# FFN tile zero of block 0 in batch columns among the AV groups; q of batches 0 and 1 in single loads, k of batch 1 moved from SP to the software ring; output weights loaded ahead of block 1's q and k

## The chip, the cores and the metric

The kernel runs on one core of one Trainium2 chip. The metric is the device time of an execution in microseconds (us). Each measurement has several executions; medians are quoted. A profiled execution gives a span that is 1.7 to 1.8 us shorter than its device time, and all times "at x us" below are counted from the start of such a span. Instruction counts and clocks come from one profiled execution per kernel.

Engines: PE is TensorE (matrix products), DVE is VectorE, ACT is ScalarE, POOL is GpSimd, SP is SyncE.

## The reference, cut to what matters

The reference is a decayed linear attention over 4 batches, 8 heads, 768 positions of 64 channels, followed by a gated FFN on the 3072 x 512 result:

```python
for b in range(nb):                                   # blocks along the sequence, one after the other
    intra = einsum('bhic,bhjc->bhij', qb, kb) * Dmask       # scores, masked by lam ** (i - j)
    intra = einsum('bhij,bhjd->bhid', intra, vb)            # "AV"
    inter = einsum('bhid,bhde->bhie', qb * lam_pow, kv_state)
    out[:, :, sl] = intra + inter
    kv_state = lam_block * kv_state + einsum('bhsd,bhse->bhde', kb_dec, vb)
# x = out, transposed to (tokens, 512)
gate = sigmoid(x @ w_gate)                            # 512 -> 1536
return (gate * (x @ w_val)) @ w_out                   # 1536 -> 512
```

The kernel works on six blocks of 128 positions, all four batches of a block together. So one block is 512 tokens: its FFN has 12 tiles of gate and value products (`gp`, `vp`: 8 matmuls of 128x512 each tile) and four output products (`po`: 12 matmuls each, one per batch).

## The kernel before

Cuts are marked with `...`. The loads at the start. `load` and `load_gv` are issued by POOL, into one queue whose descriptors POOL writes (the software ring); they cast FP32 to BF16 on the way. `load_hw` is issued by SP without a cast, so DVE casts afterwards.

```python
    load_hw("k", 0, nc.sync)                 # k of block 0, batch 0: FP32 by SP
    load_hw("k", 1, nc.sync)                 # batch 1
    nc.scalar.dma_start(out=lam_bc, ...)
    load(0, "q", 0, 2)                       # q of block 0, batches 0-1: ring
    ...                                      # memsets on DVE; a select for the identity on POOL
    nc.gpsimd.iota(ip1, ...)                 # table work on POOL
    load(0, "k", 2, 4)
    ...                                      # two more iotas, the triangle select
    load(0, "q", 2, 4)
    load(0, "v", 0, 2)
    load(0, "v", 2, 4)
    load_gv(0, 1); load_gv(1, 2); load_gv(2, 4); load_gv(4, 6)   # WG and WV, by tiles of 128 columns
```

The start on the engines: transposes of q and k (`tq`, `tk`), decay of q on DVE (`QS`), copy of k on ACT (`KS`), scores (`sp`), mask product on DVE (`MT`), AV (`op`), copy to the FFN's input (`XT`). `zeros(m)` are m filler matmuls that keep PE busy while it waits.

```python
    for b in range(2, 4):
        piece_s(0, [b]); piece_m(0, b)
    for b in range(2):
        piece_a(0, [b]); piece_x(0, [b], nc.scalar)
    zeros(3)
    piece_a(0, [2]); piece_x(0, [2], nc.scalar)
    zeros(1)
    piece_a(0, [3]); piece_x(0, [3], nc.vector)
    zeros(2)
```

Tile 0 of the FFN then needs all four batches of XT. The later loads, and the order of work for block 0 and block 1 (`trans`: transposes; `att`: AV and XT; `piece_c`: state update products; `kd`: decay of k):

```python
    load_gv(6, 8)
    load(1, "k", 0, 2); load(1, "q", 0, 2)
    load_gv(8, 10)
    load(1, "k", 2, 4); load(1, "q", 2, 4)
    load_gv(10, 12)
    load(1, "v")
    load_wo(0, 6); load_wo(6, 12)
    load(2, "kq")
    ...
    behind[7] = [trans(1, 0)]                # block 1's attention behind FFN tiles 7 to 11 of block 0
    behind[8] = [pair(piece_s, 1, 0), m_(1, 0), m_(1, 1)]
    behind[9] = [trans(1, 1), kd(1, 0)]
    behind[10] = [pair(piece_s, 1, 1), m_(1, 2), m_(1, 3), kd(1, 2), kd(1, 4)]
    behind[11] = [kd(1, 6), att(1), pair(piece_c, 1, 0), pair(piece_c, 1, 1)]
    for ft in range(NFT):
        gv(0, ft, *behind[ft])
    ...                                      # block 1: gv(1, 0..3), then po(0, 0..3), then gv(1, 4..11)
```

PSUM has five buffers for attention (two per batch of scores, one per batch of AV) and three for the FFN.

## Time and profile before

| | before |
|---|---|
| device time, median | 232.91 us (232.73 to 232.94) |
| span of the profiled execution | 231.2 us |
| PE busy | 221.5 us, 96% |
| gate product of tile 0, block 0, starts | 16.52 us |
| gate product of tile 1, block 0, starts | 18.24 us |
| first gate product of block 1 | 44.55 us |
| first output product of block 1 | 79.56 us |

The top of the profile page of the kernel before:

```profile
span 231.2 us, 3734 instructions
PE 221.5 (96%) x1483; PEld 110.6 (48%) x1508; DVE 109.5 (47%) x183; ACT 92.8 (40%) x175; POOL 47.0 (20%) x55
```

PE is nearly always busy. What can be won is in the first 17 us, where PE waits or runs filler, and in single waits later. The timeline of PE in the kernel before, at the last transposes of block 0's inputs and at the first FFN tiles (columns: start, duration, engine, line, operation, out<-in, shapes, count, and in brackets the idle time before it and what ended it):

```profile
10.85 0.62 PE L178 MATMUL tq<-ident,qb 128*128 128x128 bf16 x8 [0.39 <-DMA qb<-in_q_dram]
...
16.52 1.02 PE L273 MATMUL gp<-XT,WG 128*128 128x512 bf16 x4 [0.34 <-DVE XT L246]
17.38 1.03 PE L279 MATMUL vp<-XT,WV 128*128 128x512 bf16 x4
18.24 1.03 PE L273 MATMUL gp<-XT,WG 128*128 128x512 bf16 x4
```

Tile 0 waits for the last XT cast; then a tile takes 1.73 us. The same view where block 1's attention ends:

```profile
39.26 0.62 PE L216 MATMUL sp<-QS,KS 64*128 64x128 bf16 x16
39.81 1.04 PE L273 MATMUL gp<-XT,WG 128*128 128x512 bf16 x4
...
41.55 1.06 PE L230 MATMUL op<-QS,Sb 128*128 128x128 bf16 x16
42.53 1.08 PE L236 MATMUL op<-MT,vb 128*64 128x128 bf16 x32
43.55 1.07 PE L252 MATMUL cp<-vb,kd 128*128 128x128 bf16 x16
44.55 1.02 PE L273 MATMUL gp<-XT,WG 128*128 128x512 bf16 x3
```

Between the last scores (39.26) and AV (41.55) stands FFN tile 11. It gives DVE time for the mask products, so AV, the state products and block 1's first gate product follow without a gap: 3.00 us from 41.55 to 44.55. Duration columns overlap because matmuls are pipelined; read the starts.

The transfers, from the DMA view of the kernel before, 3 to 12 us in 40 slices of 0.225 us (first line: busy share of the 16 DMA engines; second: GB/s written):

```profile
DMA  5999999999999999999999999999999999999999
GB/s 130 213 273 291 288 288 258 203 187 177 170 158 157 158 153 153 146 152 155 160 156 155 158 155 155 151 160 158 158 155 155 158 155 155 158 159 155 156 154 155
```

SP's two loads of k run first. From 5.5 us on the ring alone moves about 155 GB/s (146 to 170).

### The profile page before, as it was taken

The page shows a single profiled execution, that of the slowest core. Times are in us where ns is not written, and L with a number is a line of the kernel's source. Part 1 is how long each engine was busy: PE and PEld are TensorE (multiplying, and loading weights), DVE is VectorE, ACT ScalarE, POOL GpSimd, SP SyncE. Part 2 cuts the span into 40 slices and gives each one's busy share as a digit, 9 for nine tenths or more (in the row PEclk, how much of TensorE's full clock was granted, in tenths as well). Part 3 has the DMA queues.
Part 4 walks back from the last instruction along what each step waited for, and adds up shares of the span by engine and source line. Part 5 has one row for each costly group of instructions (what it writes and reads, how often), then busy time and mean ns, then how long its engine had stood idle before and what let it go on. Part 6 is the DMA issues. An engine that isn't in the chain of part 4 may idle for free.

```text
span 231.2 us, 3734 instructions
## 1 busy us (share of the span) xinstructions
PE 221.5 (96%) x1483; PEld 110.6 (48%) x1508; DVE 109.5 (47%) x183; ACT 92.8 (40%) x175; POOL 47.0 (20%) x55
## 2 busy tenths in 40 slices
PE   6889999999999999999999999999999999999993
PEld 2544555644444644444644544644544554444442
DVE  3963668971068401978300978400778600333300
ACT  5557347532225823347433327442333342433220
POOL 7977672000530080026000030000000000000000
PEclk9999999999999999999999999999999999999999
DMA  7999999999799889969922967012100002100022
GB/s 114 156 176 195 173 173 176 207 168 174 209 166 164 170 94 189 224 129 114 157 53 108 209 43 52 1 45 94 45 0 0 3 35 101 48 0 0 0 91 93
DMA packets 103473, 25.15 MB, mean 109 GB/s; under 512 B 93600, under 2 KB 100512, under 8 KB 103456
## 3 DMA queue, kind: packets, MB, share of 16 engines
q0 software_dynamic: 80992, 13.90, 77.0%
q1 hardware_dynamic: 22320, 11.01, 18.5%
q8 instruction: 12, 0.20, 0.3%
q14 instruction: 5, 0.04, 0.0%
q10 hardware_dynamic: 144, 0.00, 0.0%
HBM read 28.32 MB, written 6.29 MB: 150 GB/s over the span
## 4 chain that ended last, share of the span: by engine, by line
PE 78%; DMA 13%; DVE 3%; POOL 3%; issue 2%; POOLq 0%
PE po L290 27%; PE vp L279 22%; PE gp L273 21%; DMA WV<-in_moe_w_val_dram 10%; DMA vb<-in_v_dram 3%; PE op L236 2%; PE sp L216 2%; DVE Sb L260 2%; PE op L230 2%; PE cp L252 2%; DVE ht L282 1%; POOL qb L78 1%; POOL vb L78 0%; POOL kb L78 0%; POOL WV L85 0%
## 5 line engine op out<-in xcount | busy, mean ns | idle before, releaser
L282 DVE TENSOR_TENSOR ht<-sg,vp 128x512 bf16<-128x512 bf16 x72 | 49.4, 687 | 102.6 <-PE vp L279 101.0
L279 PE MATMUL vp<-XT,WV 128*128 128x512 bf16 x282 | 73.4, 379 | 1.0 <-DMA WV<-in_moe_w_val_dram 0.3
L273 PE MATMUL gp<-XT,WG 128*128 128x512 bf16 x277 | 72.8, 379 | 0.9 <-DVE XT L246 0.3
L276 ACT ACTIVATE sg<-gp 128x512 bf16<-128x512 f32 x72 | 43.0, 597 | 74.1 <-PE gp L273 72.0
L290 PE MATMUL po<-WO,ht 128*128 128x512 bf16 (+1 forms) x294 | 62.7, 370 | 0.4 <-issue 0.2
L279 PEld LDWEIGHTS <-WV 128*128 128x128 bf16 x288 | 28.0, 98 | 34.8 <-DMA WV<-in_moe_w_val_dram 0.9
L290 PEld LDWEIGHTS <-ht 128*128 128x128 bf16 x300 | 29.0, 98 | 32.5
L273 PEld LDWEIGHTS <-WG 128*128 128x128 bf16 x288 | 26.8, 98 | 31.4 <-issue 1.8
L295 ACT COPY ob<-po 128x512 f32<-128x512 f32 (+1 forms) x24 | 13.9, 578 | 45.7 <-PE po L290 45.7
L224 DVE TENSOR_TENSOR MT<-sp,mask 128x512 bf16<-128x512 f32 x48 | 30.4, 682 | 0.6 <-PE sp L216 0.5
L98 ACT ACTIVATE kd<-kb,kds 128x256 bf16<-128x256 bf16 x40 | 17.8, 497 | 0.0
L260 DVE SCALAR_TENSOR_TENSOR Sb<-Sb,dec,cp 64x256 bf16<-64x256 bf16 x32 | 15.3, 478 | 0.8
L361 POOL COPY gates<-kt 128x1 bf16<-128x1 bf16 x4 | 0.8, 188 | 69.9 <-DMA kt<-kb 69.9
L246 ACT CAST XT<-op 128x512 bf16<-128x512 f32 x21 | 11.0, 596 | 7.1 <-PE op L236 7.0
L78 POOL DMA_DIRECT2D qb<-in_q_dram x8 | 11.5, 1441 | 3.5 <-issue 1.6
L78 POOL DMA_DIRECT2D vb<-in_v_dram x7 | 10.7, 1533 | 2.6 <-issue 1.4
L78 POOL DMA_DIRECT2D kb<-in_k_dram x7 | 10.2, 1459 | 1.5 <-DMA WV<-in_moe_w_val_dram 0.7
L304 PE MATMUL zps<-Sb 128*128 128x512 bf16 x22 | 7.8, 482 | 2.1 <-DVE Sb L123 2.1
L236 PE MATMUL op<-MT,vb 128*64 128x128 bf16 x192 | 7.1, 221 | 0.4 <-DVE MT L224 0.4
L236 PEld LDWEIGHTS <-vb 128*64 128x64 bf16 x192 | 5.7, 109 | 1.6 <-DMA vb<-in_v_dram 0.4
L252 PEld LDWEIGHTS <-kd 128*128 128x128 bf16 x80 | 5.1, 98 | 2.0
L252 PE MATMUL cp<-vb,kd 128*128 128x128 bf16 x80 | 5.9, 219 | 0.1
(42 smaller groups left out, 77.3 us busy)
## 6 DMA issues: line engine op xcount, KB each, us to landing
out_dram<-ob SPq DMA_DIRECT2D x23, 256.0 KB, 2.0
vb<-in_v_dram POOLq DMA_DIRECT2D x5, 512.0 KB, 7.9
kb<-in_k_dram POOLq DMA_DIRECT2D x4, 512.0 KB, 10.6
qb<-in_q_dram POOLq DMA_DIRECT2D x4, 512.0 KB, 12.7
WO<-in_moe_w_out_dram POOLq DMA_DIRECT2D x2, 768.0 KB, 16.7
WG<-in_moe_w_gate_dram POOLq DMA_DIRECT2D x5, 256.0 KB, 9.6
WV<-in_moe_w_val_dram POOLq DMA_DIRECT2D x5, 256.0 KB, 10.2
qb<-in_q_dram POOLq DMA_DIRECT2D x4, 256.0 KB, 8.4
```

What stands on the lines that cost most here:

```text
L78: nc.gpsimd.dma_start(out=T_[c, n][:, b0:b1], in_=src[b0:b1, :, sl, :].rearrange("b h s d -> s (b h) d"))
L98: nc.scalar.mul(KD[n][:, :, h, :], T_["k", n][:, :, h, :], kds[:, h:h + 1])
L224: nc.vector.tensor_tensor(out=MT[n, b][:, u], in0=SP[n, b][u], in1=mask[:, u], op=ALU.mult)
L236: nc.tensor.matmul(OP[n, b][us, hp, :], lhsT=T_["v", n][:, b, 2 * hp + u, :], rhs=MT[n, b][:, u, hp, :], start=(n == 0 and hp == 0), stop= ...
L252: nc.tensor.matmul(cp[:, b, :], lhsT=KD[n][:, b, 2 * hp:2 * hp + 2, :], rhs=T_["v", n][:, b, 2 * hp:2 * hp + 2, :], start=(b == 0), stop=( ...
L260: nc.vector.scalar_tensor_tensor(out=Sb[us, :, hp, us], in0=Sb[us, :, hp, us], scalar=dec[us, hp:hp + 1], in1=cp[us, :, us], op0=ALU.mult, ...
L273: nc.tensor.matmul(gp, lhsT=WG[:, mt, fs], rhs=x[:, mt, :], start=(mt == 0), stop=(mt == NMT - 1))
L276: nc.scalar.activation(sg, gp, AF.Sigmoid)
L279: nc.tensor.matmul(vp, lhsT=WV[:, mt, fs], rhs=x[:, mt, :], start=(mt == 0), stop=(mt == NMT - 1))
L282: nc.vector.tensor_mul(HT[n, ft], sg, vp)
L290: nc.tensor.matmul(po[:, :c1 - c0], lhsT=HT[n, ft][:, tt * 128:(tt + 1) * 128], rhs=WO[:, ft, c0:c1], start=(ft == 0), stop=(ft == NFT - 1))
L295: nc.scalar.copy(ob[:, c0:c1], po[:, :c1 - c0])
```

## The change

Its intent is to start the FFN sooner: FFN tile 0 is built by columns as the batches of XT arrive, the ring takes over k of batch 1 (which saves a cast on DVE) and q comes in single batches so that the first can be used sooner, and all weights precede block 1's inputs, so that block 0's FFN can run through to its output products. Block 1's attention moves from among the FFN tiles to among the output products.

```diff
     load_hw("k", 0, nc.sync)
-    load_hw("k", 1, nc.sync)
     nc.scalar.dma_start(out=lam_bc, in_=lam.partition_broadcast(128))
-    load(0, "q", 0, 2)
+    load(0, "q", 0, 1)
     ...
     make_identity(nc, ident, nomemset=True)
+    load(0, "k", 1, 2)
+    load(0, "q", 1, 2)
     nc.gpsimd.iota(ip1, ...)
-    load(0, "k", 2, 4)
+    load(0, "q", 2, 4)
     ...                                     (two iotas, the triangle select)
-    load(0, "q", 2, 4)
+    load(0, "k", 2, 4)
     load(0, "v", 0, 2)
...
+    def piece_gv_cols(n, ft, steps):        (gate and value products of one tile, by batch columns,
+        ...                                  with other work between them)
...                                          (the start's order: q before k, fewer fillers)
-    zeros(3)
-    piece_a(0, [2]); piece_x(0, [2], nc.scalar)
-    zeros(1)
-    piece_a(0, [3]); piece_x(0, [3], nc.vector)
     zeros(2)
+    piece_gv_cols(0, 0, [("g", 0, 2), last(2, nc.scalar), ("v", 0, 2), last(3, nc.vector),
+                         ("g", 2, 3), ("v", 2, 3), ("g", 3, 4), ("v", 3, 4)])
...
     load_gv(6, 8)
+    load_gv(8, 10)
+    load_gv(10, 12)
+    load_wo(0, 6)
+    load_wo(6, 12)
     load(1, "k", 0, 2)                      (then q 0-2, k 2-4, q 2-4, v of block 1)
...
-    behind[7] = [trans(1, 0)]               (and the rest of block 1's attention behind tiles 8 to 11)
+    for ft in range(1, NFT):
+        gv(0, ft, *behind[ft])
+    po(0, 0)
+    po(0, 1, trans(1, 0), kd(1, 0))
+    po(0, 2, pair(piece_s, 1, 0), m_(1, 0), m_(1, 1), trans(1, 1), kd(1, 2))
+    po(0, 3, pair(piece_s, 1, 1), m_(1, 2), m_(1, 3), kd(1, 4), kd(1, 6), att(1),
+       pair(piece_c, 1, 0), pair(piece_c, 1, 1))
...                                          (block 1: tiles 0 to 11 in a row)
```

`last(b, eng)` is AV and the XT copy of batch b.

More of the change, by code (lines that the diff above doesn't have):

```diff
@@ L282, in piece_gv, with piece_gv_cols @@
         nc.vector.tensor_mul(HT[n, ft], sg, vp)
+    def piece_gv_cols(n, ft, steps):
+        fs = slice(ft * 128, (ft + 1) * 128)
+        x = XT[n]
+        ps = {g: ps_ff.tile([128, B, C], FP32, name=g + "p", tag="ff") for g in "gv"}
+        begun = set()
+        for st in steps:
+            if callable(st):
+                st()
+                continue
+            g, b0, b1 = st
+            w = WG if g == "g" else WV
+            for mt in range(NMT):
+                nc.tensor.matmul(ps[g][:, b0:b1, :], lhsT=w[:, mt, fs], rhs=x[:, mt, b0:b1, :],
+                                 start=(g not in begun), stop=(b1 == B and mt == NMT - 1),
+                                 skip_group_check=True)
+                begun.add(g)
+        sg = htp.tile([128, TCH], BF16, tag="sg", name="sg", bufs=3)
+        nc.scalar.activation(sg, ps["g"].rearrange("p b c -> p (b c)"), AF.Sigmoid)
+        HT[n, ft] = htp.tile([128, TCH], BF16, tag="ht", name="ht", bufs=2 * NFT)
+        nc.vector.tensor_mul(HT[n, ft], sg, ps["v"].rearrange("p b c -> p (b c)"))
     def piece_po(n, tt, cuts=(0, 512)):
@@ L304, in zeros @@
             nc.tensor.matmul(zps, lhsT=Sb[:, 0, 0, :], rhs=Sb[:, 0], start=True, stop=True)
-    zeros(9)
+    zeros(8)
+    cast_hw("k", 0)
     for b in range(2):
-        cast_hw("k", b)
-        t_("k", 0, [b])
-        e_k(0, [b])
-        zeros(3 if b == 0 else 0)
-    make_mask()
-    for b in range(2):
-        t_("q", 0, [b])
-        e_q(0, [b])
+        if b == 0:
+            t_("q", 0, [b])
+            e_q(0, [b])
+            t_("k", 0, [b])
+            e_k(0, [b])
+            make_mask()
+            zeros(2)
+        else:
+            t_("k", 0, [b])
+            e_k(0, [b])
+            t_("q", 0, [b])
+            e_q(0, [b])
+    tables_late()
     zeros(1)
@@ L319 @@
         piece_m(0, b)
+    zeros(2)
+    t_("q", 0, [2, 3])
+    e_q(0, [2, 3])
+    zeros(2)
     t_("k", 0, [2, 3])
@@ L322 @@
     zeros(2)
-    t_("q", 0, [2, 3])
-    e_q(0, [2, 3])
-    tables_late()
-    zeros(3)
     for b in range(2, 4):
@@ L332, with last, go @@
         piece_x(0, [b], nc.scalar)
-    zeros(3)
-    piece_a(0, [2])
-    piece_x(0, [2], nc.scalar)
-    zeros(1)
-    piece_a(0, [3])
-    piece_x(0, [3], nc.vector)
-    zeros(2)
+    zeros(2)
+    def last(b, eng):
+        def go():
+            piece_a(0, [b])
+            piece_x(0, [b], eng)
+        return go
+    piece_gv_cols(0, 0, [("g", 0, 2), last(2, nc.scalar), ("v", 0, 2), last(3, nc.vector),
+                         ("g", 2, 3), ("v", 2, 3), ("g", 3, 4), ("v", 3, 4)])
     for n in range(2):
@@ L345 @@
     load_gv(6, 8)
+    load_gv(8, 10)
+    load_gv(10, 12)
+    load_wo(0, 6)
+    load_wo(6, 12)
     load(1, "k", 0, 2)
     load(1, "q", 0, 2)
-    load_gv(8, 10)
     load(1, "k", 2, 4)
     load(1, "q", 2, 4)
-    load_gv(10, 12)
     load(1, "v")
-    load_wo(0, 6)
-    load_wo(6, 12)
     load(2, "kq")
@@ L409 @@
         behind[ft] = [kd(0, 2 * ft)]
-    behind[4] = [pair(piece_c, 0, 0)]
-    behind[5] = [pair(piece_c, 0, 1)]
-    behind[7] = [trans(1, 0)]
-    behind[8] = [pair(piece_s, 1, 0), m_(1, 0), m_(1, 1)]
-    behind[9] = [trans(1, 1), kd(1, 0)]
-    behind[10] = [pair(piece_s, 1, 1), m_(1, 2), m_(1, 3), kd(1, 2), kd(1, 4)]
-    behind[11] = [kd(1, 6), att(1), pair(piece_c, 1, 0), pair(piece_c, 1, 1)]
-    for ft in range(NFT):
-        gv(0, ft, *behind[ft])
+    behind[5] = [pair(piece_c, 0, 0)]
+    behind[6] = [pair(piece_c, 0, 1)]
+    for g in behind[0]:
+        g()
+    for ft in range(1, NFT):
+        gv(0, ft, *behind[ft])
+    po(0, 0)
[3 more added lines that the diff above has]
+       pair(piece_c, 1, 0), pair(piece_c, 1, 1))
     for n in range(1, NSTEP):
@@ L438 @@
         if n == 1:
-            for ft in range(4):
-                gv(1, ft, *[lambda: next_loads(2)] if ft == 3 else [])
-            for tt in range(B):
-                po(0, tt, *[lambda: next_loads(3)] if tt == 3 else [])
-            gv(1, 4, *more[3])
-            gv(1, 5)
-            gv(1, 6, *more[4])
-            gv(1, 7, *more[5])
-            gv(1, 8, *more[6])
-            gv(1, 9, *more[7])
-            gv(1, 10, *more[8])
-            gv(1, 11, *more[9], *more[10], *more[11])
-        else:
-            for ft in range(NFT):
-                gv(n, ft, *more[ft])
+            more[2].append(lambda: next_loads(2))
+            more[8].append(lambda: next_loads(3))
+        for ft in range(NFT):
+            gv(n, ft, *more[ft])
         for tt in range(B):
```

## The prediction

> **What bounds the kernel now.** The page: TensorE (PE) is busy 221.5 of 231.2 us at full granted clock; the chain of waits is 78% PE, 13% DMA. Timeline, windows: FFN tile 0 of block 0 starts at 16.52 us. From there to 44.55 PE is busy 27.60 of 28.05 us, then to block 1's first output product (79.56) 34.42 of 35.01; later blocks take 35.5 to 35.7 each. Before 16.5, the software ring sets the pace (landings: q of batches 0-1 7.42, k 2-3 9.14, q 2-3 10.80, v 12.62 and 14.13, first weights 14.90 and 15.61), and VectorE, busy 4.5 to 4.7 of every 5 us.
>
> **Removed.** One VectorE cast of k (1.05 us), five filler matmuls; FFN tile 0's wait for all four XT batches (the tile is 1.73 us of PE: 8 x 216 ns); the 0.33 us wait for WV at 38.29 (weights now precede block 1's q and k).
>
> **Added or moved.** k of batch 1 (128 KB written) joins the ring, which moves 256 KB per 1.7 us: 0.83 us more before v and the weights; less contention returns perhaps 0.3. The Trainium skill ("DMA: Bandwidth & Descriptors", Issuing engines are not separate DMA queues) says that all issuers run on the same 16 DMA engines, so the move makes no bandwidth; the trace agrees: the ring gets going only as SP's packets end (4.3 to 5.4 us). Estimated landings: q0 6.1, k1 7.0, q1 7.8, q2-3 9.6, k2-3 11.3, v 13.1 and 14.6, WG0 15.4, WV0 16.1.
>
> *Start.* Batch 0's mask product moves from 9.16 to about 8.9. Batches 2-3 now wait for k, then transposes 0.6, copy 0.55, scores 0.4: mask products at about 12.9, not 12.71. The column pieces wait for WG0 and the last XT. Tile 1 starts at about 18.3, against 18.24: the later ring takes back the overlap. WV of tiles 2-3 (20.76, needed 20.83 before) may cost 0.3.
>
> *Middle.* Tiles 1-11 run without block 1's attention, then four output products. WO lands by 39.5 (estimate), just in time; block 1's k, q, v at 41 to 50, before use.
>
> *New wait.* Block 1's last scores, mask products and AV follow each other with no FFN tile between. Two batches' mask products take VectorE 2.5 us, score buffers free as they run, two XT casts (0.65 each) follow. From scores' end to block 1's first gate product: about 3.95 us, against 2.8 of pure PE work (0.89 + 1.01 + 0.90): 1.1 lost. Before, tile 11 hid this. After it nothing changes.
>
> **Sum.** Start 0.05, WV 0.3, WV at 38 -0.33, bubble 1.1, other waits -0.3: about +0.8 us.
>
> **Predicted 233.7 us, range 232.0 to 235.2.** Faster by over 2%: 0.02; within 2%: 0.96; slower: 0.02.
>
> **Tests.** k 2-3 landing later than 10.8, v and WG0 later by 0.3 to 0.6. Tile 1's first gate product at 18.0 to 18.6; first mask product at 8.6 to 9.1. At about 52 to 56 us, 1 us of idle PE released by mask products or XT. No wait for WO over 0.5. Block 1's first output product at about 80.4, and from there 151.6 to the end, as before.
>
> **What would make it wrong.** If the ring starts earlier with its half-size first load, or landings don't move, tile 1 starts by 17.7 and the change gains. If the column pieces serialise on the whole XT tile, or WO lands after 40, it loses 1 to 2 more. Bubble hidden: 232.5.

## The result and the profile after

| | before | after |
|---|---|---|
| device time, median | 232.91 us | 235.33 us (234.82 to 235.67) |
| ratio of the mean of the fast runs | | 1.0104, 95% interval 1.0084 to 1.0124 |
| span of the profiled execution | 231.2 us | 233.7 us |
| first weights of the gate (WG of tile 0) land | 14.90 us | 16.54 us |
| WV of tiles 2-3 lands | 20.76 us | 22.45 us |
| gate product of tile 1, block 0, starts | 18.24 us | 19.66 us |
| first output product of block 1 starts | 79.56 us | 81.99 us |

Ratios here and below are the mean time of one kernel's fast runs over that of the other's of the same rounds, so they are not quite the ratio of the medians. The change made the kernel 2.4 us slower, one per cent, and the result lies 0.13 us above the predicted range. From block 1's first output product to the end both traces take 151.6 to 151.7 us, so all of the loss lies before it: 1.42 us before tile 1 of block 0, and 1.01 us between there and block 1's first output product (81.99 - 19.66 = 62.33, against 79.56 - 18.24 = 61.32).

The top of the page after:

```profile
span 233.7 us, 3779 instructions
PE 223.3 (96%) x1519; PEld 111.0 (47%) x1519; DVE 108.6 (46%) x182; ACT 92.6 (40%) x175; POOL 48.4 (21%) x57
```

The timeline of PE after, at the last transposes of block 0's inputs and at the first FFN tile:

```profile
12.49 0.62 PE L179 MATMUL tk<-ident,kb 128*128 128x128 bf16 x8 [1.32 <-DMA kb<-in_k_dram]
...
16.58 0.61 PE L297 MATMUL gp<-XT,WG 128*128 128x256 bf16 x4 [0.67 <-DMA WG<-in_moe_w_gate_dram]
17.12 0.41 PE L237 MATMUL op<-MT,vb 128*64 128x128 bf16 x8
17.47 0.61 PE L297 MATMUL vp<-XT,WV 128*128 128x256 bf16 x4
...
19.21 0.38 PE L297 MATMUL gp<-XT,WG 128*128 128x128 bf16 x4 [0.23 <-DVE XT L247]
...
19.66 1.03 PE L274 MATMUL gp<-XT,WG 128*128 128x512 bf16 x4
```

The column pieces do run among the AV groups, as intended. But the first one is released by the load of WG, at 16.58 us: the start now waits for the ring. From there the chain to tile 1 has a fixed length: AV of batch 2, value columns, AV of batch 3, its XT cast, the last columns, 3.12 us from the landing of WG to tile 1 (19.66 - 16.54). It was 3.11 to 3.12 us in every other trace with these column pieces in this order in which WG gated them. The length belongs to the order: in e8 below, with AV of batch 2 ahead of the first piece, it is 2.27 us (17.14 - 14.87).

The transfers after, in the same DMA view and stretch as shown of before:

```profile
DMA  9999999999999999999999999999999999999999
GB/s 263 258 178 130 134 134 110 95 89 103 137 135 132 133 139 148 132 71 80 76 100 122 142 148 157 159 138 102 92 81 100 106 115 149 144 154 157 156 156 156
```

The rate falls to about half three times, near 4.7, 7.0 and 9.5 us. The first line stays at 9 all the while, so a low supply of packets doesn't show in it: read the GB/s. What POOL did meanwhile, from its timeline after:

```profile
1.25 1.01 POOL L78 DMA_DIRECT2D qb<-in_q_dram  x1 [0.81 <-POOLq L499]
2.36 0.30 POOL masks.py:199 TENSOR_SCALAR_AFFINE_SELECT ident<-ident 128x128 bf16<-128x128 bf16 x1
2.60 0.90 POOL L78 DMA_DIRECT2D kb<-in_k_dram  x1
3.49 0.88 POOL L78 DMA_DIRECT2D qb<-in_q_dram  x1
4.37 0.27 POOL L127 IOTA ip<- 128x128 f32 x1
4.56 1.18 POOL L78 DMA_DIRECT2D qb<-in_q_dram  x1
```

One batch (128 KB written) costs POOL 0.88 to 1.01 us to issue; the ring moves it in 0.83 us (256 KB per 1.7 us in the trace of before). Two batches cost 1.16 to 1.19 us to issue, for 1.7 us of transfer. By this count three single-batch loads in a row can't keep the ring full. That this is the cause of the dips is not shown, though, and two findings speak against it as the whole cause. If one counts the ring's packets in order (1,024 of 128 bytes a batch), the dips near 7.0 and 9.5 us fall into q and k of batches 2-3, which POOL had issued by 5.74 and 7.32 us. And in e6 below six single-batch loads in a row kept the ring nearly full once it had started. DVE isn't the cause of the dip near 7.0 us either: in e10 below it stood idle from 4.83 to 8.34 us, and the rate fell to 63 GB/s.

The timeline of PE after, where block 1's attention ends:

```profile
52.87 0.62 PE L217 MATMUL sp<-QS,KS 64*128 64x128 bf16 x16
53.42 0.40 PE L231 MATMUL op<-QS,Sb 128*128 128x128 bf16 x4
54.05 0.38 PE L231 MATMUL op<-QS,Sb 128*128 128x128 bf16 x4 [0.22 <-DVE MT L225]
54.64 0.38 PE L231 MATMUL op<-QS,Sb 128*128 128x128 bf16 x4 [0.21 <-DVE MT L225]
55.24 0.38 PE L231 MATMUL op<-QS,Sb 128*128 128x128 bf16 x4 [0.22 <-DVE MT L225]
...
57.58 1.02 PE L274 MATMUL gp<-XT,WG 128*128 128x512 bf16 x4
```

From the end of the scores to block 1's first gate product it is now 4.16 us (53.42 to 57.58) for the work that took 3.00 before. Each batch's state part of the output waits for a mask product of DVE, though it doesn't read one: by the count of PSUM buffers (four for two batches of scores, one free) it waits for a score buffer, and DVE frees those one mask product at a time. The bracketed idle times, 0.2 us each, are less than what is lost, because the ends of matmuls are modelled: the starts stand 0.6 us apart where a group of four needs 0.22.

### The profile page after: what moved, and what is told of

Same layout as the page of the kernel before. It is cut to its first block, busy times and chain, and to the rows that moved or that the text cites. A ratio compares the mean times of both kernels' runs of the same rounds, so it can differ in the third digit from the quotient of the medians.

```text
span 233.7 us, 3779 instructions
## 1 busy us (share of the span) xinstructions
PE 223.3 (96%) x1519; PEld 111.0 (47%) x1519; DVE 108.6 (46%) x182; ACT 92.6 (40%) x175; POOL 48.4 (21%) x57
## 4 chain that ended last, share of the span: by engine, by line
PE 85%; POOL 5%; DMA 4%; DVE 4%; issue 1%; POOLq 0%
PE po L312 27%; PE vp L280 25%; PE gp L274 24%; DMA WV<-in_moe_w_val_dram 4%; PE sp L217 2%; PE op L237 2%; DVE Sb L261 2%; PE cp L253 2%; PE op L231 2%; POOL qb L78 1%; DVE ht L283 1%; POOL vb L78 1%; POOL WG L84 1%; POOL WV L85 1%; DVE MT L225 1%
## 5 line engine op out<-in xcount | busy, mean ns | idle before, releaser
L283 DVE TENSOR_TENSOR ht<-sg,vp 128x512 bf16<-128x512 bf16 x71 | 48.6, 686 | 92.1 <-PE vp L280 91.5
L277 ACT ACTIVATE sg<-gp 128x512 bf16<-128x512 f32 x71 | 42.4, 597 | 74.2 <-PE gp L274 74.0
L312 PE MATMUL po<-WO,ht 128*128 128x512 bf16 (+1 forms) x300 | 63.5, 371 | 0.0
L78 POOL DMA_DIRECT2D kb<-in_k_dram x8 | 11.1, 1390 | 9.4 <-issue 8.8
L78 POOL DMA_DIRECT2D qb<-in_q_dram x9 | 12.1, 1349 | 2.8 <-issue 2.0
L326 PE MATMUL zps<-Sb 128*128 128x512 bf16 x19 | 7.0, 486 | 2.1 <-DVE Sb L122 2.1
L231 PE MATMUL op<-QS,Sb 128*128 128x128 bf16 x80 | 5.8, 219 | 0.7 <-DVE MT L225 0.7
L186 DVE TENSOR_TENSOR QS<-tq,lamq 128x1024 bf16<-128x1024 bf16 (+1 forms) x5 | 2.9, 579 | 7.1 <-PE tq L179 5.9
```

Of the source, the lines that this page charges most:

```text
L78: nc.gpsimd.dma_start(out=T_[c, n][:, b0:b1], in_=src[b0:b1, :, sl, :].rearrange("b h s d -> s (b h) d"))
L277: nc.scalar.activation(sg, gp, AF.Sigmoid)
L283: nc.vector.tensor_mul(HT[n, ft], sg, vp)
L312: nc.tensor.matmul(po[:, :c1 - c0], lhsT=HT[n, ft][:, tt * 128:(tt + 1) * 128], rhs=WO[:, ft, c0:c1], start=(ft == 0), stop=(ft == NFT - 1))
```

## The experiments

The theory after reading the two traces: 1.4 us are lost because the ring delivers late, about 1.2 in a bubble where block 1's attention has nothing to hide behind, and some waits differ. Rivals: the column pieces themselves cost; or the delay of the ring is only the extra bytes; or it is the splitting of the loads. Every kernel below gave correct results. Each was run beside the kernel before on the same chip (232.68 to 232.85 us median; one execution of 1318 us among those of the last run is in no figure here).

| label | median | ratio to before (95% interval) | WG of tile 0 lands | tile 1 starts | from there to block 1's first output product |
|---|---|---|---|---|---|
| before | 232.91 | | 14.90 | 18.24 | 61.32 |
| after | 235.33 | 1.0104 (1.0084 to 1.0124) | 16.54 | 19.66 | 62.33 |
| e1_start_old | 233.90 | 1.0048 (1.0036 to 1.0060) | 14.89 | 18.01 | 62.28 |
| e2_middle_old | 233.70 | 1.0045 (1.0032 to 1.0058) | 16.14 | 19.26 | 60.77 |
| e3_columns_only | 232.35 | 0.9989 (0.9977 to 1.0001) | 14.87 | 17.99 | 60.77 |
| e4_ring_only | 233.57 | 1.0036 (1.0023 to 1.0048) | 16.13 | 19.34 | 60.77 |
| e5_bytes | 236.77 | 1.0168 (1.0154 to 1.0181) | 15.78 | 22.50 | 61.00 |
| e6_issues | 233.27 | 1.0026 (1.0012 to 1.0040) | 15.75 | 18.76 | 61.29 |
| e7_no_bubble | 233.65 | 1.0047 (1.0033 to 1.0061) | 15.95 | 19.07 | 60.80 |
| e8_best1 | 233.05 | 1.0007 (0.9994 to 1.0019) | 14.87 | 17.14 | 62.32 |
| e9_k1_by_sp | 236.19 | 1.0151 (1.0132 to 1.0170) | 15.09 | 20.13 | 62.07 |
| e10_tables_later | 234.96 | 1.0097 (1.0079 to 1.0116) | 15.95 | 19.07 | 62.07 |
| e11_best2 | 231.78 | 0.9956 (0.9943 to 0.9969) | 14.89 | 17.16 | 60.78 |
| e12_k1_sp_cast_early | 233.93 | 1.0057 (1.0043 to 1.0071) | 15.12 | 18.23 | 62.07 |

Landings and starts are of the one profiled execution. The landing of the unchanged new start spread over 15.95 to 16.54 us in four traces (after, e2, e4, e7), that of the old start over 14.87 to 14.90 in five (before, e1, e3, e8, e11).

### e1, e2, e3 and e4: the change in parts

e1 takes back the start (loads and order), and keeps columns and middle:

```diff
+    load_hw("k", 1, nc.sync)
-    load(0, "q", 0, 1)
+    load(0, "q", 0, 2)
...                                          (all loads and the order of transposes as before, up to AV)
```

> The changed kernel with the loads and the order of the start as before (k of batches 0 and 1 by SP, q of 0-1, k of 2-3, q of 2-3 in the ring); the column pieces and the new middle stay. Theory (ring late by 1.67 us, plus a 1.16 us bubble in the middle, less 0.4 of waits saved): the first weights land at 14.9 and 15.6 again, WV of tiles 2-3 at 20.8, and the time falls by 1.6 to 1.7 us to about 233.7. Rival (the column pieces themselves cost the start time): the time stays within 0.5 us of 235.3.

Measured: 233.90 us, weights at 14.89 and 15.61, WV of tiles 2-3 at 20.76. As the theory has it, though a little less than the 1.6 to 1.7 us expected: the start is worth 1.43 us (235.33 - 233.90; different chips, but with before at 232.91 and 232.72).

e2 keeps start and columns, and takes back the middle and the later loads:

```diff
-    load_gv(8, 10); load_gv(10, 12); load_wo(0, 6); load_wo(6, 12)
     load(1, "k", 0, 2); ...
+    ...                                     (the order of loads as before)
-    po(0, 0); po(0, 1, trans(1, 0), ...); ...
+    behind[7] = [trans(1, 0)]; ...          (block 1's attention behind tiles 7 to 11 again)
```

> The changed kernel with the middle and the later loads of before (block 1's attention among the gate/value tiles of block 0, the output products of block 0 among those of block 1, WO last); the new start and the column pieces stay. Theory: the bubble of 1.16 us goes, the 0.33 us wait for WV at the end of the weights comes back: about 234.5. Rival (all of the loss is the start): 235.3 to 235.7.

Measured: 233.70 us, lower than expected. The middle costs 1.6 us, not 0.8: the bubble goes, and no wait for WV comes back.

e3 is the kernel before with the column pieces alone:

```diff
-    zeros(3); piece_a(0, [2]); piece_x(0, [2], nc.scalar)
-    zeros(1); piece_a(0, [3]); piece_x(0, [3], nc.vector)
     zeros(2)
+    piece_gv_cols(0, 0, [("g", 0, 2), last(2, nc.scalar), ("v", 0, 2), last(3, nc.vector),
+                         ("g", 2, 3), ("v", 2, 3), ("g", 3, 4), ("v", 3, 4)])
```

> The kernel before with the column pieces alone; loads, start and middle as before. Theory (the ring's landings, WV of tiles 2-3 at 20.8 us above all, set the pace of the first tiles): tile 1 starts 0.5 us earlier, at about 17.8, and the gain is then lost in waits for WV; time 232.6 to 232.9. Rival (the column pieces are worth what they move forward): 231.5 to 232.3. Second rival (they cost): over 233.3.

Measured: 232.35 us, 0.4 under before by the medians and 0.3 by the ratio, with an interval that just touches 1. The timeline of PE in e3, at tiles 0 and 1:

```profile
14.92 0.61 PE L296 MATMUL gp<-XT,WG 128*128 128x256 bf16 x4 [0.52 <-DMA WG<-in_moe_w_gate_dram]
...
17.99 1.03 PE L273 MATMUL gp<-XT,WG 128*128 128x512 bf16 x4
```

Even with the old loads the first column piece waits for WG. So 1.73 us of overlapped work moves tile 1 by 0.25 us only (17.99 against 18.24). The waits for WV that the expectation named were not in this trace, where WV of tiles 2-3 landed at 20.26 and was used at 20.58.

e4 is the new start alone, without column pieces and with the old middle:

```diff
+    zeros(3); piece_a(0, [2]); piece_x(0, [2], nc.scalar)
+    zeros(1); piece_a(0, [3]); piece_x(0, [3], nc.vector)
     zeros(2)
-    piece_gv_cols(0, 0, [...])
```

> The changed start alone (q by single batches, k of batch 1 in the ring, the start's new order), without column pieces and with the old middle. Theory: WV of tiles 2-3 lands at about 22.45 as in the changed kernel, 1.67 us later than before, so 234.5, the same as the new start with column pieces and the old middle. Rival (column pieces regain time): 0.5 to 1.2 us slower than that.

Measured: 233.57 us, against 233.70 with column pieces (e2): equal within 0.13 us, so column pieces regain nothing when the ring is late, as expected. The level was lower than expected, since its weights landed at 16.13 rather than 16.54 us.

The parts add up. From e3: the start costs 1.35 us (e2 - e3), the middle 1.55 (e1 - e3), the columns give 0.4 with the old start (if anything: the interval touches 1). Sum over before: -0.4 + 1.35 + 1.55 = 2.5 us, against 2.4 measured.

### e5 and e6: bytes or issues?

e5 puts k of batch 1 into the ring with no more loads than before; e6 splits three ring loads with no more bytes.

```diff
e5:
-    load_hw("k", 1, nc.sync)
-    load(0, "k", 2, 4)
+    load(0, "k", 1, 4)
e6:
-    load(0, "q", 0, 2)
+    load(0, "q", 0, 1); load(0, "q", 1, 2)          (likewise k of 2-3 and q of 2-3)
```

> The kernel before, with k of batch 1 taken from SP and put in the ring with k of 2-3 in one load of three batches: the changed kernel's extra 128 KB, but no more loads for GpSimd to issue. What counts is the landing of the first weights (14.9 us before, 16.1 to 16.5 with the changed start). Theory (the changed start is late because GpSimd issues small loads more slowly than the ring moves them, with its table work between them, so the ring runs dry): only the bytes count here, 0.83 us less some contention, so 15.4 to 15.7, and the ring's packet rate has no dips. Rival (the bytes on the ring are the whole delay): 16.1 or later. The time will rise more than the landing, by 0.5 to 1.5 us, because TensorE's order waits for k of batch 1, which now lands at about 9.7.

> The kernel before, with q of 0-1, k of 2-3 and q of 2-3 of block 0 each loaded by single batches: six loads in place of three, the same bytes in the ring. Theory (issue-bound): a single-batch load costs GpSimd about 0.9 us and the ring only 0.83, so the ring runs dry and the first weights land 0.7 to 1.2 us later, at 15.6 to 16.1; the packet rate shows dips between 4.5 and 9 us; time 0.4 to 1.2 us over before. Rival (bytes): the first weights at 14.9 as before, time unchanged.

Measured in e5: weights at 15.78, just above the theory's range and below the rival's: 0.88 us later than before, which is the extra bytes (0.83) in full. The contention that SP's missing load should return was not returned: the ring's first packet came at 3.40 us instead of 4.39, but its rate was reduced (85 to 149 GB/s between 3.7 and 7.9 us). Why isn't shown: POOL had issued the second load by 4.50 us. The time of e5 (236.77) says nothing of the ring: PE waited 3.12 us for k of batch 1, and its granted clock was then halved from 9.4 to 16.2 us.

Measured in e6: weights at 15.75, in the theory's range, and 233.27 us, 0.6 over before. But the trace doesn't show the reason that was given. The ring's rate had only small dips: counted as above, the packets of the second to sixth single-batch loads took 0.85 to 0.89 us each, close to the 0.83 of the full rate. What was late is the start: the first loads, SP's included, landed 0.5 to 0.7 us later than in before (5.71 against 5.02 us for k of batch 0 by SP). Why is open. So e6 supports "splitting costs", not "the ring runs dry by splitting alone".

### e9, e10 and e12: what in the start

e9 is the changed kernel with k of batch 1 by SP again, its cast behind the mask on DVE; e12 differs in that the cast stands directly behind that of batch 0.

```diff
     load_hw("k", 0, nc.sync)
+    load_hw("k", 1, nc.sync)
-    load(0, "k", 1, 2)
...
     cast_hw("k", 0)
+    cast_hw("k", 1)                          (e12; in e9 ahead of the transposes of k of batch 1)
```

> The changed kernel with k of batch 1 taken out of the ring and loaded by SP in FP32 again (with its cast); q still by single batches, all else as changed. Theory (the ring is late by 0.83 us for the extra bytes and by about 1.1 us or more for dips in which GpSimd has not yet issued the next load, and starts 0.95 us earlier because SP has one load less): bytes and one issue of 0.9 us go, the early start goes too; first weights at 15.0 to 15.4 instead of 16.1 to 16.5; first ring packet at 4.3 again; time about 234.3. Rival (splitting q, not k, makes the ring late): first weights still after 15.9, time within 0.4 us of 235.3.

Measured in e9: the weights at 15.09 and the ring's first packet at 4.30, as the theory has it, but the time was 236.19. The edit made a new chain: the cast stood behind the mask product on DVE, k of batch 1 reached PE at 9.2 us, and in the profiled execution, after a stretch with little PE work, the clock was halved. Two of the other three executions (236.49 and 237.20 us) have no such drop in their records and are slower still, so the clock alone doesn't explain the time. The windows view of e9, two neighbouring stretches (columns: stretch, length, busy time of PE, PE weight loads, DVE, ACT, POOL with counts, granted clock, DMA share, GB/s):

```profile
6.12:9.53 3.41, 1.39 (x16) 0.90 (x17) 1.89 (x3) 0.71 (x2) 3.41 (x5) 1.00 2.28 145
9.53:12.95 3.42, 3.42 (x33) 2.16 (x30) 2.42 (x5) 2.16 (x4) 3.42 (x5) 0.50 2.45 156
```

After a stretch with 1.39 us of PE work in 3.41, the next one ran at half the clock. So e9 answers the landing and not the time.

> The changed kernel with GpSimd's table work (two kinds of iota and the triangle select, about 0.8 us) put behind the load of k of 2-3 instead of between the ring loads: the same bytes, the same number of loads. Theory (dips while GpSimd does something else): the dips near 7 and 9.5 us shrink, the first weights land 0.5 to 0.8 us earlier, at 15.4 to 15.8; the decay tables and with them the first mask products come later (about 10.5 us), but tile 1 of block 0 still starts earlier, at about 18.1 to 18.8, and the time falls to about 234.3. Rival (the bytes alone): first weights at 16.1 to 16.5 as before the edit, time the same or worse.

e10 is the changed kernel with POOL's table work moved behind the loads:

```diff
     load(0, "k", 1, 2)
     load(0, "q", 1, 2)
-    nc.gpsimd.iota(ip1, ...)
     load(0, "q", 2, 4)
-    ...                                      (two iotas, the triangle select)
     load(0, "k", 2, 4)
+    nc.gpsimd.iota(ip1, ...)
+    ...
```

Measured: weights at 15.95, no better than the unedited start's best (15.95 in e7), and 234.96 us; two of its six executions (235.72 and 235.88) have a mean clock of 0.993, so the time is not of the loads alone. This part of the theory fell: moving the table work away didn't bring the weights out of the spread of the unedited start. The dip near 9.5 us went, but that near 7 us grew, and the e7 trace, with the table work in its old place, shows the dip near 9.5 us only faintly too.

> As the run with k of batch 1 by SP, but with its cast on VectorE directly behind that of batch 0. In that run the first weights landed at 15.09 us, yet tile 1 of block 0 started at 20.13, because the cast stood behind the mask on VectorE and k of batch 1 came to TensorE at 9.2 us. Theory (k of batch 1 in the ring is the start's whole cost; single q loads and the new order cost nothing to speak of): first weights at 15.0 to 15.3, tile 1 at 17.8 to 18.2, time 233.7 to 234.1, as with the whole start undone (233.9). Rival (the split and the order cost as well): tile 1 after 18.5 and over 234.5.

Measured in e12: weights at 15.12, tile 1 at 18.23 (0.03 outside the expected range), 233.93 us. That is e1's time, with the whole start undone (233.90), within 0.03 us. The chain of waits in e12 from 14 us on starts like this (start, duration, what):

```profile
8.71 6.41 DMA WG<-in_moe_w_gate_dram
...
15.16 0.61 PE gp L297 x4
```

WG lands at 15.12 (8.71 + 6.41) and releases the column pieces at once. The single-batch q loads, the new order of q and k and the fewer fillers are still in this kernel and cost little: 0.22 us in the traces (tile 1 at 18.23 against 18.01 in e1). So most of the start's loss is k of batch 1 in the ring: 1.4 us by the medians (235.33 - 233.93), 1.1 by the ratios (1.0104 - 1.0057). That is a bundle: 128 KB and one more load for POOL, one load less for SP, one cast less for DVE. The cast of k also changed its length for a reason that no run separates: 0.97 to 1.11 us in the traces with the start of before, 0.42 to 0.55 in all others.

### e7: the bubble

e7 is the changed kernel with the scores of block 1 moved inside an output product, so that the mask products run while PE works on it:

```diff
-    po(0, 2, pair(piece_s, 1, 0), m_(1, 0), m_(1, 1), trans(1, 1), kd(1, 2))
-    po(0, 3, pair(piece_s, 1, 1), m_(1, 2), m_(1, 3), kd(1, 4), kd(1, 6), att(1), ...)
+    po(0, 2, trans(1, 1), kd(1, 4), kd(1, 6),
+       mid={5: [pair(piece_s, 1, 0), m_(1, 0), m_(1, 1)]})      (after 5 of its 12 matmuls)
+    po(0, 3, att(1), pair(piece_c, 1, 0), pair(piece_c, 1, 1),
+       mid={4: [pair(piece_s, 1, 1), m_(1, 2), m_(1, 3)]})
```

> The changed kernel with block 1's two pairs of scores moved into the output products of batches 2 and 3 (after 5 and 4 of their 12 matmuls), and the k decay products of block 1 ahead of them: same work, but the mask products run while TensorE works on an output product. Theory: the 4.16 us from the last scores of block 1 to its first gate product fall to 2.8 to 3.0, the 0.19 us wait of the q transposes goes too: about 234.0. Rival (the middle costs for another reason, such as the later block-1 loads): 235.0 to 235.6.

Measured: 233.65 us, 1.7 under the changed kernel, a little more than expected (its start was 0.6 us earlier than in the trace of after, 19.07 against 19.66, within the spread of that start). The timeline of PE in e7:

```profile
50.13 0.62 PE L217 MATMUL sp<-QS,KS 64*128 64x128 bf16 x16
50.68 1.69 PE L314 MATMUL po<-WO,ht 128*128 128x512 bf16 x7
52.42 1.06 PE L231 MATMUL op<-QS,Sb 128*128 128x128 bf16 x16
...
55.43 1.02 PE L274 MATMUL gp<-XT,WG 128*128 128x512 bf16 x3
```

The state parts of all four batches run as one group again, and AV to first gate product takes 3.01 us (52.42 to 55.43), as before the change (3.00). From tile 1 to block 1's first output product it is 60.80 us, against 62.33 in the changed kernel.

### e8 and e11: a version made of the findings

e8 takes the old start, the column pieces with AV of batch 2 ahead of them, k's decay and the state products of block 0 earlier, WO in three loads, and e7's middle. e11 adds two repairs: block 2's q decay and scores stand one or two tiles later among block 1's tiles, and work that needs no new weights stands ahead of the waits for WV.

```diff
e8, over e1:
+    piece_gv_cols(0, 0, [last(2, nc.scalar), lambda: piece_kd(0, range(4)), ("g", 0, 2),
+                         last(3, nc.vector), ("v", 0, 2), ("g", 2, 3), ...])
+    load_wo(0, 4); load_wo(4, 8); load_wo(8, 12)
e11, over e8:
+    unit(lambda: piece_g(0, 1), pair(piece_c, 0, 0), lambda: piece_v(0, 1), kd(0, 6))
+    unit(lambda: piece_g(0, 2), lambda: piece_g(0, 3), lambda: piece_v(0, 2), lambda: piece_v(0, 3), ...)
+    later = [[], [], [], [], more[3], [], more[4], more[5], ...]      (block 1 only)
```

> A version made of what the runs so far say: loads and start as before (k of batches 0 and 1 by SP), column pieces with AV of batch 2 ahead of the first of them, k decay products and state products of block 0 earlier so that they fill the waits for weights, WO in three loads, the new middle with scores inside output products. Theory: tile 1 starts at about 17.1 us instead of 18.24, the output products of block 0 at about 37.2, block 1's first gate product at about 53.6; time 231.2 to 231.9, 0.4 to 0.6% under before. Rival (the ring paces the first tiles so strictly that nothing is won before block 1): 232.3 to 232.8.

Measured: 233.05 us, not faster than before. Tile 1 came at 17.14, as expected, and PE then waited until 18.72 for WV of tile 1. Block 1's first gate product came at 54.23, but then its order asked for block 2's transposed q too soon: by the waits view DVE waited 0.8 us for that transfer, and PE 0.7 us for DVE.

> The last version made of the findings, with two repairs read from its trace: block 2's q decay and scores placed one or two tiles later among block 1's tiles (its first scores waited 0.7 us for the transposed q), and the first state products and the gate products of tile 3 moved ahead of the WV waits of tiles 1 and 2. Theory: the first repair returns 0.8 us, the second 0.4: 231.6 to 232.0, 0.3 to 0.5% under before. Rival (the ring or the scheduler takes it back): 232.4 to 233.1.

Measured: 231.78 us, 0.44% under before (interval 0.31% to 0.57%), in the expected range. The timeline of PE in e11:

```profile
17.16 1.03 PE L275 MATMUL gp<-XT,WG 128*128 128x512 bf16 x4
18.03 0.61 PE L252 MATMUL cp<-vb,kd 128*128 128x128 bf16 x8
18.47 1.03 PE L285 MATMUL vp<-XT,WV 128*128 128x512 bf16 x4
19.34 1.89 PE L275 MATMUL gp<-XT,WG 128*128 128x512 bf16 x8
21.06 1.89 PE L285 MATMUL vp<-XT,WV 128*128 128x512 bf16 x8
```

State products and the gate product of tile 3 now stand where PE would have waited for WV. In this trace, though, WV of tile 1 landed at 17.13 us rather than at 18.68 as in e8, so how much each repair gave by itself is not separated.

## Why the prediction was right or wrong

The direction was right, and so was the bubble in the middle. The start was not: the prediction put it at +0.05 us, and it cost 1.42. In sum +0.8 us was predicted and +2.4 measured.

- **The failed step: the later weights.** The prediction put it as "0.83 us more before v and the weights; less contention returns perhaps 0.3", with WG at 15.4 us, tile 1 at 18.3 and the start at +0.05. WG landed at 15.95 to 16.54 us in four traces with that start, and tile 1 started at 19.07 to 19.66. Its estimates held for the single-batch loads (in after, q of batch 0 landed at 5.54 against 6.1 predicted, k of batch 1 at 7.00 against 7.0, q of batch 1 at 7.84 against 7.8). They failed from there on, where it let the ring move 256 KB in 1.7 us: q of 2-3 landed at 10.03 to 10.37 against 9.6, k of 2-3 at 11.85 to 12.45 against 11.3. The bytes cost what was said (e5: 0.88 us), but nothing was returned. The ring did start a full 1.0 us earlier (first packet at 3.39 against 4.39 us), which the prediction had named as a way for the change to gain; yet by 10 us it had moved 5,807 packets, and by 12.5 us 8,688, against 6,164 and 9,242 before (6,011 to 6,112 and 9,011 to 9,134 in e2, e4 and e7): the early start was lost again. The prediction counted no issue time of POOL (a single batch takes 0.88 us or more to issue and the ring 0.83 us to move), but that this is what slowed the ring is not shown. e12 shows that k of batch 1 in the ring is most of the start's loss; how the delay beyond the bytes divides between issue time and other causes stays open (e6 and e10).
- **The columns.** "The later ring takes back the overlap" was right: e2 and e4 differ by 0.13 us. With the old loads, too, WG is what tile 0 waits for, and in this order the gain is only 0.3 to 0.4 us, if any (e3). A better order brings tile 1 forward by another 0.85 us (e8: 17.14 against 17.99), but there it then waits for WV.
- **The new wait in the middle: mechanism and size right.** Predicted: 3.95 us from the scores to the first gate product, 1.1 lost. Measured: 4.16, 1.15 more than without the bubble (e7: 3.01).
- **The credits in the middle: right against the trace of before, but not steady.** The sum counted -0.33 us for the wait for WV at 38 and -0.3 for other waits. The trace of before has 0.55 us of waits (61.32 - 60.77: 0.33 for WV, 0.22 ahead of block 1's output products) that the traces of e2, e3 and e4 lack with the same middle; e6 has both again (61.29). So these waits come and go between executions, and against e3 there was nothing to be saved. What the prediction hadn't counted are 0.18 us in which the second transposes of q wait (tk to tq 0.62 us apart instead of 0.44, in after and e1; most likely for a PSUM buffer, which no run isolates) and 0.25 us for WV of tiles 2-3. Tile 1 to block 1's output product: 60.77 (e3) + 1.15 + 0.18 + 0.25 = 62.35, against 62.33 measured. From before it is 61.32 - 0.55 + 1.58, the same.
- **WO.** Predicted to land just in time, at 39.5 us. Its second half landed at 40.76, 1.3 us later than predicted, and the first output product, from 39.81, still had no wait: by estimate it needs that half only after six of its twelve matmuls, at about 41.1 (39.81 + 6 x 0.216). The loss of 1 to 2 us that the prediction tied to a landing after 40 didn't come: where the ring was on time (e1), the half landed at 39.18 and the product began at 38.11, so both had moved.
- **After block 1's output product** nothing changes: 151.6 us predicted, 151.7 in the trace. Right.
- **The Trainium skill's statement** ("DMA: Bandwidth & Descriptors", Issuing engines are not separate DMA queues) that all issuers share the 16 DMA engines agrees with the traces: the ring's first packet came at 3.39 us with one load by SP and at 4.39 with two. e12 adds the queue: moving 128 KB from SP's queue to the ring cost 1.1 to 1.4 us, because here the weights stand behind it in the ring.

## What to carry to other kernels

When work is moved forward, ask which event ends its wait: here the FFN's first tile waited for the landing of its weights, so building it by columns gave 0.3 to 0.4 us, and one more small load ahead of the weights in the same queue cost 1.1 to 1.4. An earlier first byte is not an earlier landing: here the ring's first packet came 1.0 us sooner and the weights 1.05 to 1.64 us later. And when attention is moved away from long matrix work, count what DVE must do between scores and AV: put the scores inside a product, not behind it.

## What the Trainium skill lacked or had wrong

- "DMA: Bandwidth & Descriptors", Anatomy of one DMA, calls descriptor generation small and says that many descriptors can be emitted before the cost shows. Here POOL took 0.88 to 1.01 us to issue one batch (128 KB written), 1.14 to 1.28 for two, 1.43 for three and 1.67 to 1.71 for four: about 0.6 us for a load and 0.27 for each batch. For the small loads that is longer than the transfer (0.83 us a batch).
- The same page, Specifications, gives about 1 us to the first byte for the GpSimd path, and doesn't say there from when. In the start after the change the ring's first packet came 2.1 us after POOL began its instruction (1.25 to 3.39 us) and 1.1 us after it had ended (2.26), which agrees if the end is meant; in the kernel before, with two loads of SP beside it, 3.1 us after the beginning (1.26 to 4.39).
- "TensorE: Matmul & The Clock Gate", What's actually happening, has the clock halved after at least one idle window of about 3.4 us. In e9 a stretch of 3.41 us with 1.39 us of PE work in it, its longest single idle time 1.41 us, was followed by 3.42 us at half the clock; in e5 it was 1.01 us of work before the drop at 9.4. That row doesn't say how much work an idle window may hold. Here 1.39 us was little enough, while 1.70 us in 3.41 (after, 9.12 to 12.53 us) kept the full clock.
- "Runtime: NRT & Kernel Launch", Instruction fetch mechanics, calls the cost of fetching the next 16 KB of instructions mostly hidden. The traces show a packet of 16,384 bytes in the instruction queue, of 0.89 to 0.98 us (at 16.66 us in before), and around it one load of the ring lands late: WV of tile 1 2.35 us behind the load before it in before, where the loads of the same size ahead of it are 0.72 apart. Which load is hit differed between executions (WV of tile 1 in before, e1 and e8, WG of tiles 2-3 in e3 and e7). No run tests whether the packet is the cause.
